# A two-layer FNet and GEGLU kernel on one core: the order of eight layer norms beside the second mixing, the queue of their row loads, one tile load, and which raw tiles stay in SBUF

## The chip, the core and the metric

One core of one Trainium2 chip. The metric is the device time of one execution in microseconds. TensorE (PE) multiplies, VectorE (DVE) and ScalarE (ACT) prepare operands and read results, GpSimd (POOL) does a few small operations and issues DMAs from its own queue, and SyncE (SP) issues most DMAs.

## What is computed

The input is x with 2048 rows of 512 numbers, float32. Two rounds of two sublayers follow, four layers in the kernel's counting (0 and 2 mix, 1 and 3 are the gated network):

```python
x = x + _A_ref(_layernorm(x))     # layer 0: a = z @ Wd_re.T, b = z @ Wd_im.T
x = x + _B_ref(_layernorm(x))     #          y = Ws_re @ a - Ws_im @ b
x = x + _A_ref(_layernorm(x))     # layer 1: (gelu(z @ w_gate) * (z @ w_up)) @ w_down
x = x + _B_ref(_layernorm(x))     # layers 2 and 3 the same
```

`Ws` is 2048 x 2048, `Wd` 512 x 512, the gate and up weights 512 x 1792, the down weight 1792 x 512.

## The kernel before

Every float32 operand is split into two parts, `hi` on ScalarE (line 160) and `lo` on VectorE (line 162), and each product is three matmuls of 128 x 128 by 128 x 512 (lines 217 to 219). The large products follow a Strassen-Winograd scheme with seven instead of eight products, so that operands such as `S1 = A21 + A22`, `S2 = S1 - A11`, `S3 = A11 - A21`, `S4 = A12 - S2` are made by VectorE (lines 193, 200) out of the raw tiles A11, A12, A21 and A22 of 128 x 512.

A mixing layer runs over four blocks `b` of 512 output rows. `plan` orders it: A11 and A12 of all blocks, then for each block the stage S2 (24 products), an early group with the hidden weights, the stage S4 (16 products: B22 and T4 in turn, two behind each other), and a late group. In layer 2 the blocks go in pairs, (0, 1) and (2, 3): the early group has 2 products, the late group 6, and twelve remaining products of a pair (`pair_rest`) run beside S2 of the next block, or beside layer 3 for the last pair. A pair's result is added into two wide tiles (`xwide`, made in the pool `upool`, for the pair's first block, and `wide` in `tpool` for the second) and written to DRAM by GpSimd (`pair_out`, line 927). The second block is complete and written first, when P5 ends; the first block follows when P3 ends.

`items` is the list of operands in the order of their products. `take` splits at most 7 items ahead of TensorE (`AHEAD`), and loads of raw tiles run 4 items ahead of the split (`RAW`). SBUF has 98 slots of 128 x 512, handed out in the order in which they came free, and the pools of the wide tiles have one buffer each. A product whose operand is itself a result (`need` in `cs`) stops the splitting ahead until that result is there.

Other work is put between products as a list of steps (`chores`); each step is called once after a product, more often if there are more steps than products left. In layer 2 the steps at block 2 (`NB - 2`) are layer 3's norms of the first half, `norm(i)` for eight row tiles, of blocks 0 and 1: load the tile's rows in four pieces (`x_load_mixed`, line 254), statistics and a few small instructions (lines 624 to 635), the normalization on ScalarE (line 668), a transpose on VectorE into a wide tile (line 757), and after four tiles a DMA of the wide tile to DRAM (line 760). `rows_ahead` asks for up to four tiles ahead. `paced` binds a step behind the newest split on ScalarE and VectorE. Beside the last S2, GpSimd fetches the turned tiles back (line 771), and their parts are split from the early group of block 3 on.

The order on each engine is written by a planner which simulates the program: among the instructions of an engine whose inputs it believes ready, the one that stands first in the code goes first. `issue_after` binds one instruction behind another in that order. On the chip each engine and each DMA queue works in the written order and waits at its head.

Of the kernel before, what the change touches and what calls it, by code (L numbers as in the profile page):

```python
# [44 lines left out]
MIXED = 4  # L45
PAIRED = {2: ((0, 1), (2, 3))}
BESIDE = 2
FIRST_SUMS = 9, 10
LATER = 3
LET = 5  # L50
# [6 lines left out]
def fnet_geglu(ctx: ExitStack, tc: tile.TileContext, x_in, ws, wh, wgu, wdn, wdc, whc, out):  # L57
# [133 lines left out]
    def minus(out, a, b):  # L191
        with behind("DVE"):
            nc.vector.tensor_tensor(out, a, b, op=ALU.subtract)  # L193
# [51 lines left out]
        engine.dma_start(t, rows(layer, i))  # L245
        return t

    def x_load_mixed(layer, i):

        g, n = divmod(i, NT)  # L250
        t = sb.get()
        for j in range(NT):
            r0 = j * P + n * 32
            nc.sync.dma_start(t[j * 32:(j + 1) * 32], xs[layer, g][r0:r0 + 32])
        return t

    def x_add(layer, i, t, ps, keep=False, engine=nc.gpsimd):
# [145 lines left out]
    def make_s2(layer, b, k):  # L403
        def run(a21, a22, *a11):
            a11 = a11[0] if a11 else held.pop(k)
            plus(a22, a21, a22)
            minus(a21, a11, a21)
            minus(a11, a22, a11)
            s1s[k], s2s[k], s3s[k] = a22, a11, a21
            sums_kept(layer, (b, k), {0: a11, 1: a22, 2: a21})  # L410
            return split_slot(a11)
        return run

# [2 lines left out]

    def make_s3(k):
        return lambda: plain(s3s.pop(k))

    def make_s4(layer, b, k):  # L420
        def run(a12):
# [105 lines left out]
    def mix_items(layer):  # L527
        def raw(make, *tiles):
            items.append((F32, tiles, make, None))

        for b, what in plan(layer):
            tiles = [[ws[(b * 2 + m) * NS + k] for k in range(NS)] for m in range(2)]
            (a11, a12), (a21, a22) = ((r[:NK], r[NK:]) for r in tiles)
            hold = b >= FORE[layer]
            if what == "A11":
                for k in range(NK):
                    raw(as_is if bare(layer, b, what, k) else make_a11(k) if hold else plain, a11[k])
            elif what == "A12":
                for k in range(NK):
                    raw(plain, a12[k])  # L540
            elif what == "S2":
                if layer and b == 0:
                    sparse.update(range(len(items), len(items) + 3 * NK))
                for j, (i, k) in enumerate(skewed(3)):
                    if rest_beside(layer, b) and j % BESIDE == 0:
                        items.extend(pair_items(PAIR_REST[j // BESIDE:j // BESIDE + 1]))
                    if layer and (b, k) in wss:
                        raw(plain, wss[b, k][i])
                    elif i == 0:
                        raw(make_s2(layer, b, k), a21[k], a22[k], *(() if hold else (a11[k],)))  # L550
                    else:
                        raw(make_s1(k) if i == 1 else make_s3(k))
            elif what == "S4":
                for i, k in skewed(2):
                    if layer and (b, k) in wss and i == 0:
                        raw(plain, wss[b, k][3])
                    elif i == 0:
                        raw(make_s4(layer, b, k), a12[k])
                    else:
                        raw(plain, a22[k])  # L560
            elif paired_with(layer, b):
                items.extend(pair_items(what))
            else:
                for m, c in what:
                    if layer == 0 and b == 0:
                        items.append((F32, (wh[m * ND + c],), make_hid_first(m, c), (m, c)))
                    else:
                        items.append((F32R, halves(whs[m, c]), make_hid(m, c), (m, c)))
# [163 lines left out]
    def block_steps(layer, w):  # L732

        zt, t, wide, asked = {}, {}, {}, set()
        turned = [dram.tile([P, NT * D], F32, name=f"t{layer}_{w}_{part}") for part in range(2)]

        def rows_ahead(i, n):
            r0 = w * 2 * NT
            end = 2 * NT if w else i // NT * NT + NT
            for k in range(i, min(i + n, end)):  # L740
                if (r0 + k) not in asked:
                    asked.add(r0 + k)
                    fresh["mixed", r0 + k] = x_load_mixed(layer, r0 + k)

        def norm(i):

            def run():
                r0 = w * 2 * NT
                end = 2 * NT if w else i // NT * NT + NT
                rows_ahead(i, 4)  # L750
                z = normed(layer, r0 + i, True)
                part, n = divmod(i, NT)
                if n == 0:
                    assert not sb.out("z")
                    wide[part] = tpool.tile([P, NT * D], F32, name="wide")
                to = wide[part].rearrange("p (b n t) -> p b n t", n=NT, t=32)
                nc.vector.transpose(to[:, :, n], z.rearrange("p (b t) -> p b t", t=32))
                sb.put(z)
                if n == NT - 1:
                    nc.gpsimd.dma_start(turned[part], wide.pop(part))  # L760
            return run

        def fetch(c):

            def run():
                for part in range(2):
                    v = zt[c, part] = sb.get()
                    for i in range(P // 32):
                        cols = turned[part][:, (c * 4 + i) * P:(c * 4 + i + 1) * P]
                        to = v[i * 32:(i + 1) * 32]  # L770
                        (nc.gpsimd if w == 0 else nc.sync).dma_start(
                            to.rearrange("p (j t) -> p j t", t=P), cols.rearrange("(j p) t -> p j t", p=32)
                        )
            return run

        def difference(a, b):
            v = sb.get()
            minus(v, a, b)
            return v

        def first(c):
            def run():
                v = t[f"B{1 + c // 2}1", c % 2] = zt.pop((c, 0))
                blocks[f"B{1 + c // 2}1", c % 2] = split_slot(v)
            return run

        def second(c):
            def run():
                v = zt.pop((c, 1))
                if c < 2:  # L790
                    t["B12", c] = v
                    t["T1", c] = difference(v, t["B11", c])
                    sb.put(t.pop(("B11", c)))
                else:
                    c0 = c - 2
                    t["T2", c0] = difference(v, t["T1", c0])
                    t["T3", c0] = difference(v, t["B12", c0])
                    sb.put(t.pop(("B12", c0)))
                    blocks["B22", c0] = split_slot(v)
                    sb.put(v)  # L800
            return run

        def fourth(c):
            def run():
                t["T4", c] = difference(t["B21", c], t["T2", c])
                sb.put(t.pop(("B21", c)))
            return run

        def divide(name, c):
            def run():  # L810
                blocks[name, c] = split_slot(t[name, c])
                sb.put(t.pop((name, c)))
            return run

        one = [norm(i) for i in range(2 * NT)]
        begin[layer, w] = lambda: rows_ahead(0, 3)
        two = [fetch(c) for c in range(ND)] + [first(c) for c in range(ND)] + [second(c) for c in range(ND)]
        two += [fourth(c) for c in range(2)]
        two += [divide(name, c) for name in ("T2", "T3", "T1", "T4") for c in range(2)]
        return one, two  # L820
# [18 lines left out]
    def mix(layer):  # L839
        hid, sums, chores, hid_left = {}, {}, [], [0]  # L840

        def chores_at(b):
            if b == NB - 3:
                norms, others = block_steps(layer + 1, 0)
                at = 0 if b in paired else NT
                if not at:
                    norms = [lambda: None] * NT + [paced(run) for run in norms]
                later.update(norms=norms[at:], fetches=others[:ND], others=others[ND:])
                return norms[:at]
            if b == NB - 2:  # L850
# [130 lines left out]
        def pair_groups(b, groups):  # L981
# [3 lines left out]
            if early:  # L985
                chores.extend(chores_at(b))
                hid_left[0] = 16
                if b + 1 < NB:
                    fetch_sums(b + 1)
                if pair_now[0][1] == NB - 1:  # L990
                    pair_wide_load(b, n)
            elif n and not final:
                for i in range(2):
                    pair_wide_load(pair_now[0][i], i)
            for i, (name, k) in enumerate(groups):
                if not early and not final and i == (4 if n else 2):
# [821 lines left out]
```

## Time and profile before

| | |
|---|---|
| median of 3 runs | 1626.4 us (1625.51 to 1627.57) |
| profiled execution, its time | 1626.79 us |
| its span, from the first to the last instruction | 1625.0 us |
| mean granted TensorE clock | 0.993 |
| TensorE matmuls | 6960, busy 1596.4 us |
| VectorE, ScalarE, GpSimd busy | 1188.9, 883.7, 316.8 us |
| DMA | 439.10 MB, mean 270 GB/s |

Times in the profile count from the first instruction. `s` stands for a slot, `p` for a PSUM bank, `ws` for the sequence matrix and sums kept of it, `x` for the activations in DRAM, `t` for the turned tiles in DRAM. "DVE L624 [6.82 <-DMA s<-x]" says that VectorE stood idle for 6.82 us before the instruction of line 624, and that the DMA that fills a slot from x ended it. A matmul's busy time overlaps the next one's, so a busy TensorE can still hide lost time; counts of matmuls in equal stretches show it. The line numbers are those of the kernel before.

### The profile page before, as it was taken

To read this page: it belongs to the slowest core of one execution; us is meant where nothing else is said; L and a number is where in the kernel's file an instruction comes from. 1 tells how busy PE (TensorE), PEld (TensorE's weight loads), DVE (VectorE), ACT (ScalarE), POOL (GpSimd) and SP (SyncE) were. 2 spreads that over 40 slices of the span, in tenths; PEclk is the share of its full clock that TensorE was granted. 3 is DMA by queue.
4 is the path that set the end of the run, shared out by engine and by line. 5 is a ranking of instruction groups with operands and counts; after the bars stand their busy time and mean duration, and the time that the engine had idled before them with its cause. 6 is when DMAs were issued, how large, how long until landed. Compare 5 with 4: busy or idle time off the path is not lost. (4 is left out here: it accounts for less than half of the span.)

```text
span 1625.0 us, 22837 instructions
## 1 busy us (share of the span) xinstructions
PE 1596.4 (98%) x6960; PEld 1308.7 (81%) x6960; DVE 1188.9 (73%) x2082; ACT 883.7 (54%) x1687; POOL 316.8 (19%) x529
## 2 busy tenths in 40 slices
PE   9999999999999999999999999997899999999999
PEld 6888888878888888888888888875678888888887
DVE  8998887868799785566879875977596566843564
ACT  8955565645767634556577543534453655433460
POOL 4122332442556102330030000012301100000000
PEclk9999999999999999999999999998999999999999
DMA  9888999995999899997876759777978958995445
GB/s 358 296 328 313 377 344 351 367 283 180 354 327 319 266 334 310 338 346 237 264 268 232 256 165 203 233 241 240 230 242 295 262 179 251 301 296 189 134 146 156
DMA packets 249115, 439.10 MB, mean 270 GB/s; under 512 B 29792, under 2 KB 73056, under 8 KB 247968
## 3 DMA queue, kind: packets, MB, share of 16 engines
q1 hardware_dynamic: 216624, 336.16, 64.9%
q0 software_dynamic: 29680, 99.38, 17.0%
q10 hardware_dynamic: 2688, 2.10, 0.4%
q8 instruction: 55, 0.90, 0.2%
q14 instruction: 68, 0.56, 0.1%
HBM read 340.26 MB, written 97.26 MB: 269 GB/s over the span
## 5 line engine op out<-in xcount | busy, mean ns | idle before, releaser
L218 PE MATMUL p<-s,s 128*128 128x512 f32 x2304 | 898.4, 391 | 6.6 <-DVE s L162 3.1
L219 PE MATMUL p<-s,s 128*128 128x512 f32 x2304 | 889.8, 390 | 0.0
L217 PE MATMUL p<-s,s 128*128 128x512 f32 x2304 | 853.6, 392 | 16.6 <-ACT s L160 6.4
L160 ACT ACTIVATE s<-s 128x512 fp32r<-128x512 f32 (+1 forms) x850 | 481.6, 608 | 309.8 <-DVE s L193 69.5
L162 DVE TENSOR_TENSOR s<-s,s 128x512 fp32r<-128x512 f32 (+1 forms) x850 | 535.2, 662 | 113.8 <-ACT s L160 91.3
L217 PEld LDWEIGHTS p<-s,s 128*128 128x128 f32 x2304 | 433.4, 188 | 113.1 <-ACT s L160 15.9
L218 PEld LDWEIGHTS p<-s,s 128*128 128x128 f32 x2304 | 434.0, 188 | 101.2 <-DVE s L162 6.6
L219 PEld LDWEIGHTS p<-s,s 128*128 128x128 f32 x2304 | 434.0, 188 | 90.4 <-DMA s<-wb 0.4
L197 DVE TENSOR_TENSOR s<-s,p 128x512 f32<-128x512 f32 x211 | 142.5, 683 | 166.4 <-PE p L219 143.0
L193 DVE TENSOR_TENSOR s<-s,s 128x512 f32<-128x512 f32 (+1 forms) x397 | 231.9, 605 | 17.6 <-DMA s<-ws 15.0
L204 ACT ACTIVATE s<-p 128x512 f32<-128x512 f32 x233 | 135.1, 592 | 116.4 <-PE p L219 112.8
L1295 ACT ACTIVATE s<-s 128x512 f32<-128x512 f32 x84 | 52.7, 628 | 41.1 <-DVE s L197 40.2
L1295 ACT ACTIVATE s<-p 128x512 f32<-128x512 f32 x28 | 16.7, 597 | 84.0 <-PE p L219 84.0
L668 ACT ACTIVATE s<-s,shift,rstd 128x512 f32<-128x512 f32 x60 | 48.5, 811 | 24.1 <-DVE shift L635 16.9
L326 POOL DMA_DIRECT2D wb<-s x84 | 45.9, 549 | 80.0 <-ACT s L160 57.9
L162 DVE TENSOR_TENSOR s<-xwide,s 128x512 fp32r<-128x512 f32 (+1 forms) x58 | 39.0, 682 | 25.0 <-ACT s L160 25.0
L1311 DVE TENSOR_TENSOR s<-s,p 128x512 f32<-128x512 f32 x56 | 38.3, 683 | 21.5 <-PE p L219 19.9
L927 POOL DMA_DIRECT2D x<-wide x8 | 5.2, 658 | 240.5 <-DVE wide L200 240.5
L645 POOL TENSOR_SCALAR rstd<-rstd 128x1 f32<-128x1 f32 x32 | 24.8, 775 | 121.2 <-ACT s L644 104.6
L211 ACT ACTIVATE p<-p 128x512 f32<-128x512 f32 x56 | 32.6, 584 | 25.2 <-PE p L219 24.4
L200 DVE TENSOR_TENSOR s<-s,s 128x512 f32<-128x512 f32 (+1 forms) x63 | 37.8, 599 | 9.8 <-DMA s<-ws 6.3
L160 ACT ACTIVATE s<-xwide 128x512 fp32r<-128x512 f32 (+1 forms) x58 | 35.3, 621 | 11.6 <-PE p L219 6.3
(105 smaller groups left out, 670.9 us busy)
## 6 DMA issues: line engine op xcount, KB each, us to landing
s<-ws SPq DMA_DIRECT2D x384, 256.0 KB, 5.3
s<-wb SPq DMA_DIRECT2D x294, 256.0 KB, 5.2
s<-wc SPq DMA_DIRECT2D x182, 256.0 KB, 4.6
wb<-s POOLq DMA_DIRECT2D x98, 256.0 KB, 5.2
s<-wq SPq DMA_DIRECT2D x56, 256.0 KB, 4.1
s<-wh SPq DMA_DIRECT2D x52, 256.0 KB, 6.2
wc<-s POOLq DMA_DIRECT2D x49, 256.0 KB, 5.3
s<-x SPq DMA_DIRECT2D x48, 256.0 KB, 5.5
```

Of the source, the lines that this page charges most:

```text
L160: newest["ACT"] = nc.scalar.activation(hi, src, AF.Copy)
L162: newest["DVE"] = nc.vector.tensor_tensor(lo, src, f32(hi), op=ALU.subtract)
L193: nc.vector.tensor_tensor(out, a, b, op=ALU.subtract)
L197: bank_read["DVE"] = nc.vector.tensor_tensor(out, a, b, op=ALU.add)
L204: bank_read["ACT"] = nc.scalar.activation(v, src, AF.Copy)
L217: nc.tensor.matmul(ps, ah, bh, start=start, stop=False, skip_group_check=True)
L218: nc.tensor.matmul(ps, ah, bl, start=False, stop=False, skip_group_check=True)
L219: newest["PE"] = nc.tensor.matmul(ps, al, bh, start=False, stop=stop, skip_group_check=True)
L326: nc.gpsimd.dma_start(a, f32(t))
L668: nc.scalar.activation(z, x, AF.Identity, bias=shift, scale=rstd)
L1295: nc.scalar.activation(t, g, AF.Gelu_apprx_tanh)
L1311: nc.vector.tensor_tensor(t, t, v, op=ALU.mult)
```

## The change

Three things change, in one diff.

1. In layer 2 the eight norms run in the order 4, 5, 6, 7, 0, 1, 2, 3, that is block 1 first. Rows of tiles 4 to 6 are asked for by a step of their own on GpSimd's queue, at the first step of the list; five empty steps follow (four before); rows of tiles 0 to 2 are asked for by another step of their own, on SyncE's queue, between norms 6 and 7. Both are not paced. The list grows from 12 to 15 steps, in the same 16 places.
2. The wide tile of the last block (3) is loaded at its late group instead of its early group.
3. In layer 0, blocks 1 to 3, the sum S1 gets a slot of its own, and the raw A22 tile stays in its slot until S4, which loaded it a second time before.

```diff
+WAIT = 5
+HELD = {0: (1, 2, 3), 2: ()}
...
-    def x_load_mixed(layer, i):
+    def x_load_mixed(layer, i, engine=nc.sync):
...
-            nc.sync.dma_start(t[j * 32:(j + 1) * 32], xs[layer, g][r0:r0 + 32])
+            engine.dma_start(t[j * 32:(j + 1) * 32], xs[layer, g][r0:r0 + 32])
...
             a11 = a11[0] if a11 else held.pop(k)
-            plus(a22, a21, a22)
+            s1 = a22
+            if b in HELD[layer]:
+                s1, a22s[k] = sb.get(), a22
+            plus(s1, a21, a22)
             minus(a21, a11, a21)
-            minus(a11, a22, a11)
-            s1s[k], s2s[k], s3s[k] = a22, a11, a21
-            sums_kept(layer, (b, k), {0: a11, 1: a22, 2: a21})
+            minus(a11, s1, a11)
+            s1s[k], s2s[k], s3s[k] = s1, a11, a21
+            sums_kept(layer, (b, k), {0: a11, 1: s1, 2: a21})
...
+    a22s = {}
+
+    def make_a22(k):
+        return lambda: plain(a22s.pop(k))
...
                         raw(make_s4(layer, b, k), a12[k])
+                    elif b in HELD[layer]:
+                        raw(make_a22(k))
                     else:
                         raw(plain, a22[k])
...
-        def rows_ahead(i, n):
+        def rows_ahead(i, n, engine=nc.sync):
...
-                    fresh["mixed", r0 + k] = x_load_mixed(layer, r0 + k)
+                    fresh["mixed", r0 + k] = x_load_mixed(layer, r0 + k, engine)
...
         begin[layer, w] = lambda: rows_ahead(0, 3)
+        begin[layer, w, "ahead"] = rows_ahead
...
                 at = 0 if b in paired else NT
                 if not at:
-                    norms = [lambda: None] * NT + [paced(run) for run in norms]
+                    ahead = begin[layer + 1, 0, "ahead"]
+                    norms = [paced(run) for run in norms[NT:] + norms[:NT]]
+                    norms.insert(NT - 1, lambda: ahead(0, 3, nc.sync))
+                    norms = [lambda: ahead(NT, 3, nc.gpsimd)] + [lambda: None] * WAIT + norms
...
-                if pair_now[0][1] == NB - 1:
+                if b == NB - 2:
                     pair_wide_load(b, n)
-            elif n and not final:
-                for i in range(2):
+            elif n:
+                for i in range(final, 2):
                     pair_wide_load(pair_now[0][i], i)
```

## The prediction

> **What bounds the kernel now.** The span is read in stretches of 25 us first, because an average over it hides its stages. The columns of the stretches are the stretch, its length, busy time and instructions of PE, PEld, DVE, ACT and POOL, the granted TensorE clock, the DMA share and GB/s.
>
> ```profile
> 325.00:350.00 25.00, 24.33 (x107) 19.51 (x106) 19.50 (x32) 12.84 (x23) 13.00 (x24) 1.00 1.05 331
> 350.00:375.00 25.00, 22.99 (x100) 18.27 (x99) 17.29 (x29) 14.77 (x27) 6.54 (x12) 1.00 0.75 206
> ...
> 1025.00:1050.00 25.00, 25.00 (x112) 20.68 (x111) 22.81 (x39) 13.90 (x24) 0.00 (x0) 1.00 0.66 209
> ```
>
> TensorE is the bound: where nothing stops it, 25 us hold 112 matmuls, 4.48 per us or 0.223 us each. I therefore count missing matmuls instead of idle time, since that also catches matmuls that run at a lower clock. The first mixing misses 5 + 12 in 325 to 375, 17 x 0.223 = 3.8 us. By far the most is missing near the end of the second mixing, here in finer stretches:
>
> ```profile
> 1097.00:1110.00 13.00, 10.85 (x45) 7.81 (x45) 6.12 (x16) 2.19 (x4) 1.10 (x2) 1.00 0.79 177
> 1110.00:1125.00 15.00, 8.50 (x21) 5.27 (x20) 13.86 (x36) 9.68 (x16) 3.21 (x5) 0.66 0.94 338
> 1125.00:1136.00 11.00, 8.13 (x29) 5.92 (x28) 10.76 (x23) 5.50 (x10) 5.95 (x10) 0.84 0.59 186
> ...
> 1155.00:1161.00 6.00, 5.14 (x23) 3.94 (x21) 0.00 (x0) 1.26 (x3) 3.28 (x7) 1.00 1.12 207
> 1161.00:1168.00 7.00, 1.65 (x6) 1.05 (x6) 1.62 (x3) 1.78 (x3) 3.20 (x6) 0.84 1.05 249
> 1168.00:1181.00 13.00, 12.58 (x47) 10.25 (x48) 13.00 (x23) 9.23 (x17) 0.00 (x0) 0.82 0.77 241
> ```
>
> Hole A, 1097 to 1136: 39 us would hold 174.7 matmuls, 95 ran, 79.7 are missing, 17.8 us. Hole B, 1155 to 1181: 26 us hold 116.5, 76 ran, 40.5 are missing, 9.0 us. With 3.8 us in the first mixing, 30.6 us lie where the change works; that is the ceiling of the gain.
>
> What made hole A is read on three queues. Columns: start, duration, engine and line, count, and in brackets the idle time before with what ended it.
>
> ```profile
> 1095.49 1.91 SPq L924 DMA_DIRECT2D xwide<-x  x4
> 1097.44 11.42 SPq L254 DMA_DIRECT2D s<-x  x20
> 1109.99 24.89 SPq L340 DMA_DIRECT2D s<-ws  x22
> ```
>
> ```profile
> 1065.31 2.62 POOL L927 DMA_DIRECT2D x<-wide  x4 [171.86 <-DVE wide L200]
> 1083.76 2.57 POOL L927 DMA_DIRECT2D x<-xwide  x4 [15.82 <-DVE xwide L200]
> 1105.53 0.56 POOL L631 TENSOR_TENSOR rstd<-rstd,power 128x1 f32<-128x1 f32 x1 [19.21 <-DVE rstd L630]
> ```
>
> ```profile
> 1094.98 1.37 DVE L197 TENSOR_TENSOR s<-s,p 128x512 f32<-128x512 f32 x2 [5.50 <-PE p L219]
> ...
> 1103.88 0.69 DVE L624 BATCH_NORM_STATS2 st<-s 128x6 f32<-128x512 f32 x1 [6.82 <-DMA s<-x]
> 1104.49 0.67 DVE L162 TENSOR_TENSOR s<-s,s 128x512 fp32r<-128x512 f32 x1
> 1105.08 0.17 DVE L626 BATCH_NORM_AGGREGATE mv<-st 128x2 f32<-128x6 f32 x1
> 1105.29 0.15 DVE L630 TENSOR_SCALAR rstd<-mv 128x1 f32<-128x1 f32 x1
> ...
> 1109.25 0.71 DVE L757 STREAM_TRANSPOSE wide<-s 128x512 f32<-128x512 f32 x1
> ```
>
> Block 1 of the pair goes to DRAM at 1065, block 0 only at 1084 (POOL L927). The norms begin with block 0, so the first row tile is asked for behind the xwide load at 1097.44 and the first BN_STATS stands at the head of VectorE's queue until 1103.88, 6.82 us idle after another 5.50 us idle before 1094.98. Behind it stand the splits that TensorE wants, such as the L162 at 1104.49. SyncE issues 20 row requests in one run after the xwide load, and from 1095.49 to 1109.99 not one s<-ws load for the next products. From 1110 VectorE is full (13.86 of 15, 10.76 of 11) and cannot make up for it.
>
> Hole B is a DMA matter:
>
> ```profile
> 1166.38 0.69 DVE L193 TENSOR_TENSOR s<-s,s 128x512 f32<-128x512 f32 x1 [15.05 <-DMA s<-ws]
> ```
>
> ```profile
> s<-ws SPq DMA_DIRECT2D x12, 256.0 KB, 10.6
> s<-t POOLq DMA_DIRECT2D x24, 64.0 KB, 7.5
> t<-wide POOLq DMA_DIRECT2D x1, 1024.0 KB, 5.0
> wide<-x SPq DMA_DIRECT2D x4, 256.0 KB, 11.2
> ```
>
> ```profile
> SPq L340 <- DMA wide<-x: 5.7, 3, 2.4
> ...
> SPq L924 <- DMA t<-wide: 0.7, 1, 0.7
> ```
>
> Those DMA rows are 1140 to 1170: an s<-ws load takes 10.6 us to land, beside the wide tile's 11.2 us and 24 fetches of the turned tiles, 7.5 us each. SyncE's ws loads stand 5.7 us behind the wide load.
>
> **The change, part by part.** The sum is against the profiled execution, 1626.8 us (span 1625.0 and 1.8 around it); the median of the runs, 1626.4, is 0.4 lower.
>
> *Block 1's norms first.* Eight norms stay eight. Each costs VectorE 0.69 + 0.17 + 0.15 + 0.15 + 0.71 = 1.87 us (statistics, aggregate, rstd, shift taken like rstd, transpose), 15.0 us in all. Before, none ran until 1103.88. Block 1's rows go to DRAM 18.5 us sooner (1065.31 against 1083.76), so up to three norms (5.6 us) fall into the 12.3 us that VectorE idled, and the 6.82 us at the head of its queue vanish: from 1104 on VectorE is 6.8 + 5.6 = 12.4 us ahead of where it was. The hole of 17.8 us is 2.15 + 6.50 + 2.87 = 11.5 us of idle TensorE and 6.3 us of lower clock after the stops (0.66 and 0.84 in the rows). 12.4 us cover the idle part, and the clock's part goes with it. The five empty steps and the extra ones delay the last norm by three steps; the last four (7.5 us) now fall beside short products, which is why I leave a rest. I take 13 of 17.8 us, nearer to the upper end because the head of the queue is what the rows name; the ends are 17.8 and, if the four late norms stop TensorE as the eight did, 0.
>
> *Rows by POOL's queue.* POOL's own rows for such requests, and for the turned tiles that rival 3 needs:
>
> ```profile
> 1128.65 4.37 POOL L771 DMA_DIRECT2D s<-t  x8 [1.03 <-PE p L219]
> ...
> 1141.86 0.60 POOL L760 DMA_DIRECT2D t<-wide  x1 [8.12 <-DVE wide L757]
> ...
> 1165.35 1.63 POOL L771 DMA_DIRECT2D s<-t  x3 [0.96 <-DMA s<-t]
> ```
>
> Twelve requests leave SyncE, at most 11.42 / 20 = 0.57 us each there, 6.9 us. On POOL they cost 4.37 / 8 = 0.55 us each, 6.6 us. POOL stood idle 15.82 us before 1083.76 and 19.21 us before 1105.53, so they are hidden; without that cover they stand 6.6 us in front of block 0's writes or of the first rstd, which queue behind them on POOL, and the norms wait for both. The fourth row tile of each block (8 requests, 4.6 us) and three of block 0 (12 requests, asked for by a step bound to no other instruction) stay on SyncE, so 20 of 32 remain there, and the ws loads should begin some 5 us sooner than 1109.99. That is part of the 13 us.
>
> A rule speaks against this part. The Trainium skill, "SBUF — State Buffer", section "A bandwidth-pool intuition that's wrong (but worth ruling out)", has a request from GpSimd's queue take about 3100 ns instead of about 620 ns beside a VectorE copy. By it, as an estimate, twelve would take 37 us, the first norms would come no sooner than now, A's 13 us would be lost, and the time would be 1621.4. The 0.55 us of the row, beside a VectorE busy 10.76 of 11 us, disagrees with it here.
>
> *The last wide tile later.* The request moves behind the last S4 in the code, yet it waits for no slot, only for its tile, and the 0.7 us wait on t<-wide shows that it went out the moment the tile was free. The planner may send it at that moment again. If it does move away, the 5.7 us on SyncE and the pieces go, and B closes; its four requests (about 0.5 us each) then lie at the start of the next layer. Ends 0 and 9.0 for B. I take 4, nearer to the lower half, since the fetches stay, and since block 0's tile is now the last written and its fetches have less time. Later cost at the next layer: 0 to 5.7 us by the same SyncE row, I take 1.
>
> *A22 tiles held in layer 0.* 24 loads of 256 KB (three blocks, eight tiles) leave SyncE and the DMA; the sum S1 gets a slot of its own, so 8 more slots are held from S2 to S4, and no instruction is added. Blocks 1 and 2 lose no matmuls, so 16 of the 24 loads save nothing. In block 3 the 3.8 us begin here:
>
> ```profile
> 352.78 0.69 DVE L200 TENSOR_TENSOR s<-xwide,s 128x512 f32<-128x512 f32 x1 [3.70 <-DMA xwide<-ws]
> ```
>
> and fewer loads compete with that one. Ends 3.8 and, if slots come free later, -2 (half that wait again); I take 2.
>
> Sum: 13 + 4 + 2 - 1 = 18 us; 1626.8 - 18 = 1608.8, from the median 1608.4.
>
> **A rule beside the trace.** TensorE's longest single wait in hole A:
>
> ```profile
> PE p L218 <- DVE rstd L630: 3.0, 1, 3.0
> ```
>
> The clock was 0.66 in 1110 to 1125 all the same. The Trainium skill, "TensorE: Matmul & The Clock Gate", section "What's actually happening", has the half clock follow at least one idle window of about 3.4 us. By that rule, worked as an estimate, the short stops left of A would cost no clock, and by A's split of 11.5 to 6.3 the 4.8 us that I leave would be 1.7 us smaller: 1606.7. The trace speaks for the dearer reading, which the sum uses.
>
> **The rivals.**
> 1. VectorE is the bound and the hole only moves. Its rows after 1110 are full, the eight norms still cost 15.0 us, and the last four now crowd late. Then only the 6.82 us come back, with 2 in layer 0 and nothing in B: 1626.8 - 8.8 = 1618. Against it: the 12.3 idle us that the early norms can use.
> 2. No change: only 20 of the 32 row requests stand in the run of 1097.44, so the planner already sent the others, of block 1, earlier; the wide tile goes out as before, and the first norm waits for another late row. Gain under 3 us, 1625.
> 3. Slower: the fetches of block 0 become the bound. Its turned tile is now the last written, and its four chunks are the first that are split behind the last S2. Now the second tile goes out at 1141.86 and POOL's last fetch at 1165.35 + 1.63, landing 7.5 us later at 1174. If it stays so while A's 13 us are won, TensorE comes to that place, now at hole B's 1162, at 1162 - 13 = 1149, with seven split products (7 x 6 x 0.223 = 9.4 us) in hand: 1174 - 1149 - 9.4 = 15.6 us idle, with A's share of clock (17.8 / 11.5) 24 us. 1626.8 - 13 - 2 + 24 = 1636. It decides from a second tile written later than about 1136. Against it: VectorE is 12.4 us ahead by then, which brings the tile to about 1129.
> 4. All holes close: 1626.8 - 30.6 = 1596.
>
> **How the numbers follow.** Forecast 0.61 (gain 12 to 25 us, 1602 to 1615), rival 1 0.21, rival 2 0.07, rival 3 0.07, rival 4 0.04. About 0.2% (3.3 us) is what a measurement can tell here. Faster 0.61 + 0.21 + 0.04 = 0.86, same 0.07, slower 0.07. The range leaves out rivals 2 and 3 and the outermost part of rival 4: 1597 to 1623.
>
> **What would show it.** Right: the first BN_STATS of the stage before 1100 with no wait of several us; s<-ws requests between 1095 and 1110; the granted clock at 1.00 through that stage; x rows from POOL at about 0.55 us a request. The wide load: if it is issued right when t<-wide has landed, the move did nothing, and any closing of B has another reason. In layer 0: 24 fewer s<-ws requests and more than 107 and 100 matmuls in 325 to 375. Wrong: VectorE idle before a transpose that waits for its wide tile, POOL's write of block 0 later than 1090, or a new wait of TensorE at the start of the fourth layer.

## The result, and the profile after

The kernel after takes 1610.9 us (median of 4 runs, 1610.0 to 1612.1) where the kernel before beside it takes 1626.1: the ratio is 0.9906, with an interval of 0.9889 to 0.9923. In a later comparison the same pair gave 0.9907 (0.9890 to 0.9923). The profiled execution took 1612.14 us, 14.65 less than that of before. The forecast of 1608.4 came close; its parts did not. The stretches of after, in the columns of the prediction:

```profile
325.00:350.00 25.00, 25.00 (x112) 20.71 (x111) 23.10 (x39) 13.70 (x25) 9.19 (x18) 1.00 0.97 318
350.00:375.00 25.00, 25.00 (x112) 20.67 (x112) 19.21 (x33) 14.77 (x27) 9.84 (x19) 1.00 0.64 207
...
1097.00:1110.00 13.00, 12.61 (x56) 10.12 (x54) 13.00 (x30) 7.21 (x12) 2.55 (x3) 1.00 0.85 169
1110.00:1125.00 15.00, 8.50 (x24) 6.42 (x24) 8.73 (x23) 4.76 (x8) 3.22 (x5) 0.77 0.72 242
1125.00:1136.00 11.00, 7.36 (x23) 5.88 (x24) 10.72 (x21) 6.53 (x12) 6.70 (x13) 0.69 0.70 205
1155.00:1161.00 6.00, 6.00 (x29) 4.95 (x27) 6.00 (x11) 2.42 (x5) 3.06 (x6) 1.00 1.05 303
1161.00:1168.00 7.00, 7.00 (x31) 5.55 (x30) 4.75 (x9) 6.02 (x12) 0.00 (x0) 1.00 1.02 309
1168.00:1181.00 13.00, 13.00 (x58) 10.51 (x56) 13.00 (x22) 3.98 (x7) 0.00 (x0) 1.00 0.93 322
```

Counted as before, by missing matmuls of 0.223 us: 325 to 375 misses none now (3.8 us back). Hole B misses none (9.0 back). Hole A ran 56 + 24 + 23 = 103 of 174.7 and still misses 71.7, or 16.0 us (1.8 back). Together 14.6 us. That this equals the difference of the two executions is partly chance: a matmul that crosses the border of two stretches counts in both, and in 400 to 425 after runs 108 matmuls where before ran 111. The start times of the 6960 matmuls in the two traces give it without stretches: after is 2.3 us ahead where hole A begins, 5.1 where it ends, 14.0 behind hole B and 14.4 at the end, so A gave 2.8 and B 8.9. A also differs between executions of the same kernel: in that of the later comparison, after_again, it ran 59 + 33 + 23 = 115 and misses 13.3 us (4.5 back). So the hole that was to give most, 13 us, gave 2 to 5.

What is left of A are two stops. The waits of TensorE from 1097 to 1140 (engine and line, what it waited for, us in total, times, longest):

```profile
PE p L220 <- DVE s L164: 6.6, 1, 6.6
PE p L219 <- ACT s L162: 3.9, 1, 3.9
```

SyncE's queue, and the rows of VectorE and ScalarE in the same place:

```profile
1085.35 9.92 SPq L342 DMA_DIRECT2D s<-ws  x11
1095.45 2.08 SPq L940 DMA_DIRECT2D xwide<-x  x4
1097.58 12.44 SPq L256 DMA_DIRECT2D s<-x  x16
1110.11 11.70 SPq L342 DMA_DIRECT2D s<-ws  x12
```

```profile
1086.35 0.69 DVE L636 BATCH_NORM_STATS2 st<-s 128x6 f32<-128x512 f32 x1
...
1113.51 0.69 DVE L164 TENSOR_TENSOR s<-s,s 128x512 fp32r<-128x512 f32 x1 [2.73 <-ACT s L162]
1116.49 0.69 DVE L202 TENSOR_TENSOR s<-s,s 128x512 f32<-128x512 f32 x1 [2.29 <-PE p L221]
...
1125.28 0.69 DVE L202 TENSOR_TENSOR s<-s,s 128x512 f32<-128x512 f32 x1 [1.53 <-DMA s<-ws]
...
1127.91 0.68 DVE L164 TENSOR_TENSOR s<-s,s 128x512 fp32r<-128x512 f32 x1
...
1130.89 0.70 DVE L769 STREAM_TRANSPOSE wide<-s 128x512 f32<-128x512 f32 x1
```

```profile
1107.24 0.62 ACT L162 ACTIVATE s<-s 128x512 fp32r<-128x512 f32 x1
...
1112.85 2.19 ACT L162 ACTIVATE s<-s 128x512 fp32r<-128x512 f32 x4 [3.41 <-DMA s<-ws]
```

The first norm now starts at 1086.35 without a wait, and 11 ws loads go out ahead of the xwide load, from 1085.35, where row requests stood before. But SyncE still sends block 0's 16 row requests behind the xwide load, and the next ws load goes out at 1110.11; before it was 1109.99. That load ends ScalarE's wait at 1112.85 and makes the first stop, before the matmul of 1113.53. The second stop, 6.6 us before 1128.64, waits for the lower half of a split whose upper half ScalarE made at 1107.24: TensorE ran its first matmuls with it at 1109.00. On VectorE's written queue the lower half stands behind the statistics and small instructions of block 0's norms and behind sums whose inputs come late (the waits at 1116.49 and 1125.28), and ran only at 1127.91. VectorE is not full there: it was busy 8.73 of the 15 us from 1110, where before it was busy 13.86. It stood at the head of its queue.

Hole B, SyncE's queue of before first, then that of after:

```profile
1136.80 9.30 SPq L340 DMA_DIRECT2D s<-ws  x4
...
1150.93 13.27 SPq L340 DMA_DIRECT2D s<-ws  x8
```

```profile
1134.00 1.16 SPq L342 DMA_DIRECT2D s<-ws  x2
...
1135.99 8.24 SPq L342 DMA_DIRECT2D s<-ws  x6
1144.91 2.12 SPq L940 DMA_DIRECT2D wide<-x  x4
1148.04 7.47 SPq L342 DMA_DIRECT2D s<-ws  x7
```

And SyncE's waits there (1125 to 1170), a row of before and two of after:

```profile
SPq L340 <- DVE s L162: 18.1, 6, 5.9
```

```profile
SPq L342 <- DVE s L164: 7.3, 6, 3.3
...
SPq L940 <- DMA t<-wide: 0.6, 1, 0.6
```

The last transpose of the norms is at 1130.89, where it was at 1140.86, and SyncE waits 7.3 us for VectorE's splits instead of 18.1, so slots come free sooner there. SyncE does not wait less in all: 34.2 us in that stretch, 33.2 before, and 11.6 of them now end with a matmul of TensorE (lines 220 and 221), where before it was 2.1. What changed is how early the loads go. The last eleven ws loads of the second mixing, sent from 1150.93 to 1171.13 before, all behind the wide tile, are sent from 1136.99 to 1155.13, four of them ahead of it and seven behind. The wide tile itself still goes out the moment the turned tile has landed (0.6 us of wait).

### The profile page after: what moved, and what is told of

Same layout as the page of the kernel before. It is cut to its first block, busy times and chain, and to the rows that moved or that the text cites. A ratio compares the mean times of both kernels' runs of the same rounds, so it can differ in the third digit from the quotient of the medians.

```text
span 1610.3 us, 22810 instructions
## 1 busy us (share of the span) xinstructions
PE 1591.4 (99%) x6960; PEld 1309.3 (81%) x6960; DVE 1188.7 (74%) x2082; ACT 882.1 (55%) x1687; POOL 320.8 (20%) x541
## 2 busy tenths in 40 slices
DMA packets 245467, 432.80 MB, mean 269 GB/s; under 512 B 29408, under 2 KB 72672, under 8 KB 244320
## 4 chain that ended last, share of the span: by engine, by line
PE 91%; DMA 4%; DVE 3%; ACT 1%; issue 1%; SPq 0%; POOL 0%; DVEq 0%; ACTq 0%; POOLq 0%
PE p L219 30%; PE p L220 30%; PE p L221 30%; DMA s<-ws 2%; DVE s L164 1%; DVE s L195 1%; DMA s<-wq 1%; DMA xwide<-x 1%; PE p L1055 1%; DMA s<-x 1%; ACT s L162 0%; DVE s L199 0%; POOL rstd L657 0%; SPq L342 0%; SPq L256 0%
## 5 line engine op out<-in xcount | busy, mean ns | idle before, releaser
L202 DVE TENSOR_TENSOR s<-s,s 128x512 f32<-128x512 f32 (+1 forms) x61 | 36.6, 602 | 21.0 <-DMA s<-ws 14.4
L162 ACT ACTIVATE s<-xwide 128x512 fp32r<-128x512 f32 (+1 forms) x56 | 34.2, 617 | 26.0 <-DVE xwide L199 9.0
L657 POOL TENSOR_SCALAR rstd<-rstd 128x1 f32<-128x1 f32 x32 | 19.5, 608 | 111.0 <-ACT s L656 103.1
```

The lines of the kernel that those rows point to most:

```text
L162: newest["ACT"] = nc.scalar.activation(hi, src, AF.Copy)
```

## The experiments

All ratios are to the kernel before, run beside each; times 1626.4 they give the microseconds in brackets.

| kernel | median us | ratio (interval) |
|---|---|---|
| after, two comparisons | 1610.9, 1612.7 | 0.9906, 0.9907 (-15.2) |
| e1_norms: part 1 alone | 1620.6 | 0.9959, 0.9947 to 0.9970 (-6.7) |
| e2_held: part 3 alone | 1625.6 | 0.9985, 0.9976 to 0.9994 (-2.4) |
| e3_wide: part 2 alone | 1627.5 | 1.0002, 0.9993 to 1.0012 (0) |
| e12_held_12: after, two blocks held | 1612.7 | 0.9918, 0.9901 to 0.9934 (-13.3) |
| e5_sync: after, rows by SyncE | 1621.7 | 0.9968, 0.9958 to 0.9978 (-5.2) |
| e7b_pool_0: after, all rows ahead by GpSimd | 1624.2 | 0.9976, 0.9964 to 0.9989 (-3.9) |
| e10_xwide_late, two comparisons | 1608.6, 1609.9 | 0.9896, 0.9894 (-17) |
| e11_before_xwide_late | 1620.3 | 0.9966, 0.9955 to 0.9977 (-5.5) |
| e13_wait_3 | 1619.8 | 0.9949, 0.9931 to 0.9967 (-8.3) |
| e14_xwide_late_wait_3 | 1607.7 | 0.9874, 0.9852 to 0.9895 (-20.5) |

**The parts alone.** Each is the kernel before with one part of the diff.

> The kernel before with the first part alone: block 1's norms first, its rows asked for by GpSimd's queue, five empty steps. Theory (the norms' earlier end also closes hole B, because SyncE no longer stands waiting for slots that the last norms free, and its ws loads of block 3 go out some 9 us before the fetches and the wide tile): B closes here too, A is eased by about 3 us, layer 0 keeps its 3.9 us; 1626 - 11 = 1615, between 1613 and 1617, and in the trace the ws loads of block 3's S2 and S4 are issued before 1140. Rival (B closes because the wide tile is asked for later): B stays at about 9 us, the gain is A's 3 us, 1623.

> The kernel before with the A22 tiles held in layer 0 alone. Theory (the hole of layer 0 at 340 to 375 was made by the DMA, which had 24 loads of 256 KB too many): all of its 3.9 us come back, 1622.2, between 1621 and 1623.5, nothing changes in the second mixing. Rival 1 (the shift of the later stages changes holes A and B as well, so that the after kernel's gain there is partly this part's): below 1620. Rival 2 (slots come free later and a new wait opens): 1625 or above.

> The kernel before with the last wide tile's request moved behind the last S4 in the code, alone. Theory (the request goes out the moment its tile is in DRAM, wherever it stands in the code): 1626 within 1 us, the wide load is issued within 1 us after the landing of the turned tile as before, hole B still misses about 9 us. Rival (the move takes the burst away from the ws loads): B closes, 1618 to 1621.

The wide tile's move alone does nothing: every engine's instructions stand in the same order as before, the request follows the landing as before, and the ratio is 1.0002. The theory holds, and with it hole B has another reason than the move. The tiles held alone bring 2.4 us, less than their theory's 3.9: 325 to 375 is full (112 and 112 matmuls), but 400 to 425 ran 107 where before ran 111. The norms alone bring 6.7, less than their theory's 11 and more than their rival's 3. In its profiled execution A misses 13.3 us (59 + 42 + 14 matmuls ran), and B shrank but did not close: from 1155 to 1181 it ran 28 + 20 + 52 = 100 of 116.5 matmuls where before ran 76. That execution took 6.4 us more than the kernel's median, so its sizes are rough. One stop behind B comes from the written order; of VectorE's rows:

```profile
1188.62 1.28 DVE L198 TENSOR_TENSOR s<-s,p 128x512 f32<-128x512 f32 x2 [4.19 <-PE p L220]
```

The same place costs TensorE 3.7 us in e7b_pool_0 and 3.9 in e13_wait_3, and 0.4 in after, where VectorE does that sum (line 199) at 1176.80 and waits for nothing. The parts add up to 6.7 + 2.4 = 9.1 us, some 6 less than all together (each interval is about 2 us to either side).

**Where the missing 6 us come from.** The raw tiles held in blocks 1 and 2 alone:

```diff
-HELD = {0: (1, 2, 3), 2: ()}
+HELD = {0: (1, 2), 2: ()}
```

> The kernel after, with the A22 tiles of layer 0 held in blocks 1 and 2 only (block 3 loads them again). From the second layer on every engine's instructions stand in the same order as in the kernel after; that order differs after 1134 us from the order of the kernel with the norms alone (1620.6). Theory O (the parts do not add up to the change's gain, 6.7 + 2.5 of 15.5 us, since the tiles held shift the planned order, and the order that comes out behind 1134 us is worth the rest): the hole of layer 0 is open again (3.9 us), the rest is as in the kernel after; 1614 to 1616. Rival (the rest comes from the 24 loads that are gone, all of them): 1618 or more, since 8 of the 24 are back.

0.9918 is close to after and far from the sum of the parts. What this kernel shares with after, and e1_norms lacks, is 16 of the 24 loads that are gone, the wide tile's later request, and the written order. In the traces its engines work in after's order from 430 us on; against e1_norms the order of VectorE differs from 1140 on. Loads of layer 0 are long over at 1100. The wide tile's request, which moves nothing alone, stands among the same ws loads in e1_norms but for one; that it is worth something beside the norms was not run, and so is not excluded. B is closed here (28 + 32 + 57 = 117 matmuls), and A misses 16.0 us as after's does. So theory O is borne out, as far as a comparison of two plans goes: holding tiles in layer 0 shifts the planner's clock, and the order it then writes for the end of layer 2 is worth some 6 us. Nobody aimed at that. In layer 0 it showed something else: 325 to 375 is full (112 and 112 matmuls, 17 more than before) although block 3 loads its eight tiles again, and 400 to 425 runs 17 fewer than before. The 16 loads only move the hole of layer 0; the other eight close it. Its row, then that of after and that of before:

```profile
400.00:425.00 25.00, 22.86 (x94) 18.39 (x93) 15.81 (x31) 18.48 (x40) 14.25 (x27) 0.93 0.91 287
```

```profile
400.00:425.00 25.00, 24.25 (x108) 19.75 (x106) 16.60 (x34) 18.80 (x43) 15.78 (x28) 1.00 0.94 302
```

```profile
400.00:425.00 25.00, 25.00 (x111) 20.56 (x110) 17.90 (x35) 19.32 (x43) 18.19 (x28) 1.00 0.85 282
```

**Is SyncE's queue what keeps A open?** Block 0's rows taken off it too:

```diff
-                    norms.insert(NT - 1, lambda: ahead(0, 3, nc.sync))
+                    norms.insert(NT - 1, lambda: ahead(0, 4, nc.gpsimd))
```

> The kernel after, with block 0's four row tiles also asked for by GpSimd's queue, so that SyncE has no row request between the load of xwide and the next ws loads. Theory (what is left of hole A, 15.9 us, comes from SyncE's 16 row requests of 1097.6 to 1110.0 that stand ahead of the ws loads for block 1's products, 3.9 us of stop, and of the slots that VectorE waits for next): the ws loads go out by 1100, the first stop goes and the second gets shorter, 5 to 10 us less than the kernel after, 1601 to 1606. Rival 1 (VectorE is the bound there: eight norms and the splits fill it): less than 2 us, 1609 to 1611. Rival 2 (requests on POOL delay its rstd and writes, the norms of block 0 come later): slower than the kernel after, 1612 to 1618.

and block 1's rows given back to it:

```diff
-                    norms = [lambda: ahead(NT, 3, nc.gpsimd)] + ...
+                    norms = [lambda: ahead(NT, 3, nc.sync)] + ...
```

> The kernel after, with block 1's three row tiles asked for by SyncE instead of GpSimd's queue. Theory (12 requests of 0.4 us return to a SyncE that stands waiting for DMA lanes anyway, but they also move the loads behind them): ws loads of block 1's products are issued later by about 5 us, a stop opens before 1100; 3 to 8 us slower than the kernel after, 1614 to 1619. Rival (the queue does not matter, the norms' order does): within 2 us of the kernel after, 1609 to 1613.

Both lose about 10 us of the 15, so the theory of e7b_pool_0 fell. The direction of e5_sync's theory was right with too small a size, and not in its place: no stop opened before 1100 (1097 to 1110 ran 59 matmuls), the stops of A grew. TensorE waits 10.5 us there in after, 16.3 in e7b_pool_0 (three waits for splits of ScalarE, the longest 8.2), and 13.3 in e5_sync for the same (the longest 7.6). Of e7b_pool_0, SyncE's row, the landing times of 1097 to 1113 (KB each, median us), GpSimd's rows and the row of VectorE behind them:

```profile
1096.75 26.95 SPq L342 DMA_DIRECT2D s<-ws  x14
```

```profile
s<-ws SPq DMA_DIRECT2D x8, 256.0 KB, 8.7
s<-x POOLq DMA_DIRECT2D x8, 64.0 KB, 8.0
```

```profile
1130.03 3.26 POOL L783 DMA_DIRECT2D s<-t  x6 [0.99 <-issue]
1133.31 2.11 POOL L643 TENSOR_TENSOR rstd<-rstd,power 128x1 f32<-128x1 f32 x4
```

```profile
1133.91 0.16 DVE L647 SCALAR_TENSOR_TENSOR shift<-mv,rstd 128x1 f32<-128x1 f32 x1 [4.08 <-POOL rstd L643]
```

SyncE did send its loads sooner: the load that makes the first stop in after went out at 1100.0 instead of 1110.1. But it landed at 1110.7 instead of 1112.8; behind the pieces of xwide and the rows the loads took 8.7 us. And on GpSimd the planner now put eight fetches of the turned tile (two at 1127.92 and the six shown) ahead of block 0's four rstd, so VectorE stood 4.1 us at its head. e5_sync shows the same order, eight fetches and then the four:

```profile
1131.43 4.34 POOL L783 DMA_DIRECT2D s<-t  x8 [5.66 <-PE p L220]
1135.79 2.11 POOL L643 TENSOR_TENSOR rstd<-rstd,power 128x1 f32<-128x1 f32 x4
```

Giving the twelve requests back to SyncE thus costs 10 us, more than the 6.9 us that they take there, but I cannot say how much of that is the queue and how much the order that each variant came with.

**The burst.** The xwide load is first read at 1214 and sent at 1095. It is moved to about 1182:

```diff
-                if b == NB - 2:
-                    pair_wide_load(b, n)
...
                 step()
+                if final and not early and i == 5:
+                    with tc.issue_after(stream["last"].ins):
+                        pair_wide_load(pair_now[0][0], 0)
```

> The kernel after, with the load of the xwide tile (four requests of 256 KB, sent at 1095 us and first read at 1214 us) moved to about 1182 us; the order of every other request of SyncE and GpSimd is as in the kernel after. Theory A (what is left of hole A is made by the DMA: this 1 MB in pieces of 512 bytes stands in the rings ahead of the row tiles and of the ws loads, which is why moving the row requests to GpSimd brought nothing): the row tiles land by about 1100 and the ws load of the first stop by 1107 instead of 1112.8, the stop of 3.9 us goes, that of 6.6 us shrinks by 3 to 5; 1602 to 1605. Rival 1 (VectorE's order and its norms make the hole): within 1.5 us of the kernel after, 1609.5 to 1612.5. Rival 2 (the load is as harmful where it is sent now, among the loads of the fourth layer's start): about the kernel after or slower, with a new stop after 1182.

> The kernel after with the load of the xwide tile late, once more beside the kernel after on one chip. Theory A, as corrected by its first run (the DMA made the first stop only; what VectorE has planned ahead of the late split makes the second, which grows): 1.5 to 3 us less than the kernel after. Rival: within 1 us of it.

SyncE's queue, and TensorE's waits from 1095 to 1140:

```profile
1094.94 7.86 SPq L256 DMA_DIRECT2D s<-x  x16
1102.90 21.68 SPq L342 DMA_DIRECT2D s<-ws  x14
```

```profile
PE p L220 <- DVE s L164: 7.8, 1, 7.8
PE p L219 <- ACT s L162: 0.4, 1, 0.4
```

The time missed theory A's 1602 to 1605, though the theory is right for the first stop: the rows take 7.9 us instead of 12.4, the ws load goes out at 1102.90, and the stop of 3.9 is 0.4. The second stop grew from 6.6 to 7.8, because TensorE came to the same split sooner; there rival 1 is right. A ran 56 + 28 + 43 = 127 matmuls, 24 more than in after, or 5.4 us; B gave some of that back in this execution (106 of 116.5). The gain over after is small, 0.9896 and 0.9894 against 0.9906 and 0.9907, which the intervals do not separate.

The same move on the kernel before:

> The kernel before with the same move of the xwide load alone: the norms still begin with block 0 and all rows are asked for by SyncE. Theory A (the load makes much of hole A): the first norm comes some 4 to 6 us sooner, hole A shrinks from 18 us by 6 to 10; 1616 to 1621. Rival (hole A is made by the late write of block 0 at 1084 and by VectorE's eight norms after it): less than 3 us, 1624 or more.

5.5 us, inside the theory's range, but in another place: A still misses 17.1 us (51 + 28 + 19 matmuls ran) and B closes (116 ran). Part of that is lost again: 1180 to 1200 ran 73 where before ran 83. The first norm came 3.4 us sooner (1100.43). The burst costs before too, but its hole A was not made by it.

**VectorE's order.** Three empty steps instead of five put that split 25 instructions further ahead on VectorE:

```diff
-WAIT = 5
+WAIT = 3
```

> The kernel after with three empty steps ahead of the norms instead of five. On VectorE's planned queue the split for which TensorE stops longest (6.6 us at 1128.6 in the kernel after) then stands 25 instructions further ahead, before most of block 0's norms. Theory V (that stop is VectorE's own order: the split's upper half lies ready from 1108.8, and the work planned ahead of it, statistics and transposes of four norms among it, lets it run at 1127.9 only): the stop shrinks to 2 us or less; 1606 to 1609. Rival (the turned tile of block 0, written later, sends the fetches and the wide load later, and hole B opens again): the stop shrinks but 3 us or more stand at 1160 to 1180; 1610 to 1615.

> The kernel after with both: the load of the xwide tile at about 1182 us (which took away the stop of 3.9 us and left one of 7.8 us behind the same split of VectorE) and three empty steps instead of five. Theory V: the remaining stop goes too, hole A is below 5 us, 1601 to 1605, the fastest so far. Rival (hole B opens again): 1606 to 1611.

> The kernel after, unchanged, beside the three variants: 15 us less than the kernel before, ratio 0.9906 within 0.0015.

For e13_wait_3, TensorE's waits from 1095 to 1130, a row of VectorE, and the two late stretches:

```profile
PE p L219 <- ACT s L162: 8.4, 2, 7.1
PE p L220 <- DVE s L164: 2.1, 1, 2.1
```

```profile
1113.97 0.69 DVE L164 TENSOR_TENSOR s<-s,s 128x512 fp32r<-128x512 f32 x1 [5.62 <-ACT s L162]
```

```profile
1155.00:1180.00 25.00, 21.84 (x84) 17.16 (x83) 18.18 (x30) 10.44 (x19) 0.00 (x0) 0.86 0.80 252
1180.00:1200.00 20.00, 16.07 (x64) 12.81 (x63) 17.13 (x29) 11.02 (x20) 0.00 (x0) 0.91 0.59 206
```

No wait for a split of VectorE is longer than 2.1 us now, as theory V says. But a ws load that the planner had now put behind the rows made a stop of 7.1, and 28 + 26 matmuls (12 us) are missing from 1155 to 1200, 3.9 us of it behind the sum named under e1_norms. So the rival decides, and by more than it said: 7 us slower than after, 1619.8 where it had 1610 to 1615. With the burst moved as well, e14_xwide_late_wait_3 has only short stops left in A:

```profile
PE p L220 <- DVE s L164: 6.5, 3, 3.4
```

It misses 10.4 us there (51 + 30 + 47 ran) and is the fastest kernel here, 0.9874 against after's 0.9907 in the same comparison; the intervals overlap a little. It fell short of theory V's 1601 to 1605, as some of hole B came back (96 of 112 matmuls from 1155 to 1180). Moving the burst brings about 2 us in the plan of after and 12 in that of e13_wait_3: its price depends on the plan, and on which loads are written behind it.

## Why the prediction was right, and where it was wrong

- **The sum** (18 us, measured 14.65 in the executions) held by luck: two terms that were too small stand beside one that was too large, and what was worth some 6 us, by the runs a changed order of the plan, was in no term.
- **Block 1's norms, 13 of 17.8 us: wrong, 1.8 (4.5 in after_again).** The lead of VectorE is real: no wait before the first statistics, the last transpose 10.0 us sooner, of which about 2.3 is layer 0's. The step that failed is that 12.4 us of lead cover A's idle part. The idle part was 11.5 us before and is 10.5 in after, and the clock's part stayed with it (0.77 and 0.69 in the rows). TensorE waited there for a ws load, which no lead of VectorE sends sooner, and for one split, which stood on VectorE's queue behind block 0's norms, now the late ones; the lower end of this term had named that. That the ws loads would begin 5 us sooner failed by itself: the 12 requests left SyncE, but the load stayed at 1110.11, since the requests at its head waited for the burst (3.1 us of such waits, and 2.98 us for the first row request alone).
- **The lead paid in hole B: 9.0, where I took 4.** I had written that a wide load sent at once would mean that "any closing of B has another reason". It was sent at once; slots of VectorE's splits came free sooner, and the last loads went out 14 to 16 us sooner, where TensorE came 5.1 us sooner. With the norms alone B went from 76 to 100 of 116.5 matmuls, so part of its closing came with the changed order.
- **Tiles held, 2: measured 3.8 in place, 3.1 with what 400 to 425 loses, 2.4 alone.** The 24 loads are gone (439.10 MB before, 432.80 after). "16 of the 24 loads save nothing" held for the time of layer 0: without them the hole at 325 to 375 only moves to 400 to 425. The effect that I had no term for is the planner's: about 6 us from a changed order some 700 us later. e12_held_12 speaks for it; it compares two plans and cannot exclude every other difference between them.
- **-1 at the start of the fourth layer: not seen.** After runs 151 of 156.8 matmuls from 1165 to 1200, before 146 of 152.3 in the same place, 1181 to 1215.
- **Rows by GpSimd, hidden: right.** The prediction's 0.55 us a request is 0.50 here, 3.95 us for the first eight, and block 0's write came at 1081.82, 1.9 us sooner than before, while TensorE was some 2.4 us ahead there by layer 0:

```profile
1073.02 3.95 POOL L256 DMA_DIRECT2D s<-x  x8 [7.49 <-DMA s<-wq]
...
1081.82 2.66 POOL L943 DMA_DIRECT2D x<-xwide  x4 [0.57 <-DVE s L164]
```

  VectorE was busy for the whole of 1073 to 1082. The Trainium skill, "SBUF — State Buffer", section "A bandwidth-pool intuition that's wrong (but worth ruling out)", has about 3.1 us a request beside a copy (`tensor_copy`) of VectorE. VectorE's rows of 1073 to 1082 are tensor_tensor work and a transpose, so they neither bear that out nor speak against it; the prediction was wrong to set its row, which stood beside no copy either, against the rule.
- **The rivals.** Rival 1, a full VectorE, is not what remains of A: VectorE was idle for 6.3 of the 15 us from 1110. What remains is its order, and a load. Rival 3 put its point at a second turned tile later than about 1136. It went out at 1136.49, and nothing stopped; TensorE had not gained A's 13 us, so it also came to the place later than the rival has it.

## What to carry to other kernels

In these runs a lead that an engine gained was paid where the next wait that ended last depended on it, and not where the engine had looked idle: name for each stop the one load or split that ends it, and ask whether the change moves that one. A transfer that is needed late but sent as soon as its source is ready can take the rings from loads that are needed now; bind it to a later point. With a planner that writes the queues, each edit, even one far away, changes the order elsewhere, so parts measured alone need not add up; compare the written orders before giving a gain to an edit.

## What was not expected of the hardware

A request that is sent sooner lands little sooner when a burst stands in the rings: the load of e7b_pool_0 that went out 10.1 us sooner landed 2.1 us sooner. From 1097 to 1113 the ws loads took a median of 8.7 us to land in e7b_pool_0 and 3.0 in e10_xwide_late, where the burst is gone. The row pieces took 8.0 us from GpSimd's queue beside the burst. From SyncE's they took 2.0 beside it (after) and 1.9 without it: there the wait stands ahead of the request, 12.4 us for 16 of them instead of 7.9.

The clock fell to half without any long wait. Of e13_wait_3, TensorE's rows and then two stretches:

```profile
1163.76 0.73 PE L219 MATMUL p<-s,s 128*128 128x512 f32 x2 [1.81 <-ACT s L162]
1165.84 2.07 PE L219 MATMUL p<-s,s 128*128 128x512 f32 x4 [1.35 <-ACT s L188]
```

```profile
1162.00:1166.00 4.00, 0.89 (x3) 0.46 (x3) 3.20 (x6) 3.44 (x7) 0.00 (x0) 0.83 0.69 236
1166.00:1172.00 6.00, 6.00 (x16) 4.69 (x17) 6.00 (x11) 4.58 (x9) 0.00 (x0) 0.55 0.47 133
```

Two waits of 1.81 and 1.35 us, 3.1 us of 4 idle, and the next 6 us ran at 0.55, 16 matmuls where 27 fit. In these rows two short stops close together cost the clock as one long stop does. The prediction weighed the rule of the Trainium skill, "TensorE: Matmul & The Clock Gate", section "What's actually happening", by which the half clock follows an idle window of about 3.4 us. If that window must be wholly idle, these rows disagree, as those of before did at a longest wait of 3.0 us.
